# The output staging tile of the second channel matmul: two buffers or three

## Chip, cores, metric

One core of one Trainium2 chip. The metric is device time in microseconds (us) of one execution, median over several executions. On one core a run counts as slow when it lies over 1.5% above the fastest of the same kernel.

## The reference, cut to what matters

Cosine attention over 8 batches, 12 heads, 448 rows, head size 64, followed by a token-and-channel mixer on the 448 x 768 result of each batch.

```python
q_n = q / (norm(q) + 1e-6);  k_n = k / (norm(k) + 1e-6)
attn = softmax(q_n @ k_n.T / tau)
x = (attn @ v)                       # laid out as batch, 448, 768
h = relu(x.T @ w_tok1) @ w_tok2      # token mixing
u = x + h.T
h2 = relu(u @ w_ch1) @ w_ch2         # channel mixing, hidden size 1536
out = u + h2                         # float32
```

The change touches only the last line: the sum `u + h2` and its way to memory.

## The kernel before

The program runs 48 head pairs through a software pipeline (the loop index `i` below is one pair) and feeds the channel matmuls of finished batches into it piece by piece. The buffers:

```python
outp = ctx.enter_context(tc.tile_pool(name="outp", bufs=2))     # the staging tile
ps = ctx.enter_context(tc.tile_pool(name="ps", bufs=2, space=PSUM))   # two banks: psF, psG, pst, some psU
ps2 = ctx.enter_context(tc.tile_pool(name="ps2", bufs=3, space=PSUM))
```

The second channel matmul, its eviction and its store. Matmuls write into PSUM, a memory of its own that is split into banks; the eviction is the VectorE instruction (L407) that adds the residual to such a result and puts the sum into the staging tile. Each output tile holds 128 rows of 768 float32 (3 KiB a partition) and is filled in two halves, `i0:i1` = 0:3 and 3:6:

```python
def m_ch2(b, m, i0, i1, send=False):
    ...
    if i0 == 0:
        ost[0] = outp.tile([P, D], FP32, name=f"ost_{b}_{m}", tag="ost")
        ost[1] = 0
    o, w = ost[0], P * (i1 - i0)
    psF = ps.tile([P, DH], FP32, name=f"psF_{b}_{m}_{i0}", tag="b")
    for ct in range(CT):                       # 12 matmuls               (L404)
        nc.tensor.matmul(psF[:, 0:w], gt[:, ct, lo:lo + P], wc2t[:, ct, P * i0:P * i1], ...)
    nc.vector.tensor_tensor(out=o[...], in0=psF[...], in1=urt[b][...], op=ALU.add)   # eviction (L407)
    if send or i1 == DT:
        if m < NC:
            nc.sync.dma_start(out=out[b, 0:SM]...[m][:, cols], in_=o[:, cols])       # store (L414)
        else: ...                              # the 64 + 64 remainder rows of two batches (L416, L417)
```

Loads, transposes and stores are all issued from one queue, SyncE's, in program order:

```python
for i in range(NP_ALL + 2):
    if i < DMA_FROM:
        loads(i)                  # q, k, v of later pairs (q: L106, k: L109, v: L112)
    if DMA_FROM <= i + 2 < NP_ALL:
        dma_tpose(i + 2)          # query/key transposes (L265)
    ...
    for p in ut_at.get(i, ()):
        u_tpose(p)                # transposes of the residual (L380)
    ...
    feed(...)                     # channel matmuls, evictions and stores, among scores and attention
```

## Time and profile before

| | before |
|---|---|
| median of the first three runs | 394.86 us (394.48 to 395.2) |
| span of the profiled run | 392.9 us |
| TensorE busy | 378.7 us (96%) |
| VectorE busy | 193.5 us (49%) |
| evictions into the staging tile | 57 (28 tiles) |
| of these, held by a store | 1, for 3.4 us |

In a timeline line the columns are start in us from the span's start, length in us, engine, source line, operation, output and inputs, count; in brackets stands how long the engine was idle before it and what released it. "SPq" is the queue that issues the transfers; a line there is the issue, not the moving of the bytes. In a list of waits the columns are who waited for whom, us in total, times, longest.

The prediction shows the main lines. Two more of the kernel before belong to the argument. First, the waits of the issuing queue between 82 and 100 us:

```profile
SPq L106 <- POOL kq L211: 7.4, 1, 7.4
```

A query load (L106) held the queue for 7.4 us, because its buffer was still being read by GpSimd's scaling (L211). Everything behind it in the queue waited too: two transposes, and then the first store, whose tile was full at 82.31, 4.06 us before the load could go out at 86.37. Second, a table by stretches, of 86 to 100 us and 100 to 360 us: for each engine busy us and instructions in brackets, in the order TensorE, weight loads, VectorE, ScalarE, GpSimd; then granted clock, DMA share, GB/s.

```profile
86.00:100.00 14.00, 12.72 (x114) 7.46 (x113) 7.50 (x13) 4.21 (x6) 12.72 (x19) 1.00 1.02 227
100.00:360.00 260.00, 259.85 (x2535) 157.14 (x2534) 117.86 (x232) 145.78 (x247) 136.30 (x191) 1.00 0.77 163
```

TensorE idles 1.28 us in the first stretch and 0.15 us in the 260 us after it.

### The profile page before, as it was taken

How to read it: one execution, taken by the hardware profiler on the slowest of the kernel's cores; microseconds unless marked ns; L12 is line 12 of the kernel's file. 1: busy time of each engine (PE TensorE's matmuls, PEld its weight loads, DVE VectorE, ACT ScalarE, POOL GpSimd, SP SyncE). 2: the span in 40 equal slices, each digit the busy share in tenths (PEclk: the TensorE clock that was granted, in tenths of full speed). 3: DMA queues.
4: the chain of work that ended last, by engine and by line, in shares of the span. 5: the costliest groups of instructions: out<-in, count | busy, mean ns of one | idle time of the engine just before them, and what ended most of it. 6: DMA issues, size and time to landing. Idle time of an engine off the chain costs nothing.

```text
span 392.9 us, 9076 instructions
## 1 busy us (share of the span) xinstructions
PE 378.7 (96%) x3658; PEld 228.5 (58%) x3658; DVE 193.5 (49%) x368; ACT 225.8 (57%) x411; POOL 209.6 (53%) x306
## 2 busy tenths in 40 slices
PE   8678999998999999999999999999999999999996
PEld 3346555665565656566556566566566566565554
DVE  5688758865344554545524645345534342333022
ACT  5998698843774639573676446673775536511400
POOL 4978486789267584868572947659561700000000
PEclk9899999999999999999999999999999999999999
DMA  7999999969968987999989899999982452013013
GB/s 203 276 238 253 246 236 215 227 138 264 209 131 190 202 183 179 222 183 208 205 199 198 175 245 216 166 189 182 242 142 56 123 123 68 16 57 102 5 40 120
DMA packets 137514, 67.51 MB, mean 172 GB/s; under 512 B 93248, under 2 KB 134016, under 8 KB 137472
## 3 DMA queue, kind: packets, MB, share of 16 engines
q1 hardware_dynamic: 133296, 61.36, 71.4%
q0 software_dynamic: 3632, 5.18, 7.4%
q8 instruction: 28, 0.46, 0.5%
q10 hardware_dynamic: 544, 0.39, 0.3%
q14 instruction: 14, 0.11, 0.1%
HBM read 43.38 MB, written 11.01 MB: 138 GB/s over the span
## 4 chain that ended last, share of the span: by engine, by line
PE 86%; ACT 6%; DVE 3%; DMA 2%; SPq 1%; issue 1%; ACTq 0%; DVEq 0%
PE psF L404 28%; PE psG L389 27%; PE psO L320 9%; PE psS L301 7%; PE psR L341 5%; PE psU L361 4%; ACT pt L302 3%; PE psO L322 3%; PE psX L308 2%; DMA out_dram<-ost 1%; DMA km<-in_k_dram 1%; PE psU L366 1%; PE pst L243 1%; ACT sq L178 1%; DVE ost L407 1%
## 5 line engine op out<-in xcount | busy, mean ns | idle before, releaser
L302 ACT ACTIVATE pt<-psS 128x896 f16<-128x896 f32 x141 | 119.0, 921 | 65.8 <-PE psS L301 65.5
L389 PE MATMUL psG<-ut,wc1t 128*128 128x448 f16 x576 | 119.5, 353 | 0.2
L404 PE MATMUL psF<-wc2t,gt 128*128 128x384 f16 (+2 forms) x684 | 117.3, 324 | 1.2 <-DVE ost L407 1.1
L391 ACT ACTIVATE gt<-psG 128x448 f16<-128x448 f32 x96 | 51.1, 557 | 73.2 <-PE psG L389 73.2
L404 PEld LDWEIGHTS <-gt 128*128 128x128 f16 x684 | 64.5, 98 | 48.4 <-issue 8.1
L389 PEld LDWEIGHTS <-wc1t 128*128 128x128 f16 x576 | 53.2, 98 | 52.5 <-issue 8.7
L211 POOL TENSOR_TENSOR kq<-km,rn 128x384 f16<-128x384 f32 x47 | 39.4, 837 | 80.9 <-ACT rn L204 80.7
L407 DVE TENSOR_TENSOR ost<-psF,ur 128x384 f32<-128x384 f32 (+2 forms) x57 | 31.4, 550 | 90.0 <-PE psF L404 86.6
L320 PEld LDWEIGHTS <-pt 128*128 128x128 f16 x1152 | 50.1, 97 | 8.4 <-issue 2.4
L320 PE MATMUL psO<-vt,pt 128*128 128x65 f16 x1152 | 52.4, 193 | 1.2 <-ACT pt L302 0.8
L326 DVE RECIPROCAL rec<-psO 128x8 f32<-128x8 f32 x48 | 9.9, 207 | 80.9 <-PE psO L322 80.9
L193 DVE TENSOR_REDUCE ssq<-sq 128x12 f32<-128x768 f32 (+1 forms) x49 | 45.1, 929 | 5.3 <-ACT sq L178 3.7
L322 PE MATMUL psO<-vx,pt 128*128 128x130 f16 x192 | 41.8, 218 | 0.0
L180 POOL TENSOR_TENSOR sq<-km 128x384 f32<-128x384 f32 x42 | 34.5, 823 | 13.2 <-DMA km<-in_k_dram 13.0
L211 POOL TENSOR_TENSOR kq<-qm,rn 128x384 f16<-128x384 f32 x47 | 39.5, 841 | 0.0
L301 PE MATMUL psS<-qk 64*128 64x448 f16 x282 | 36.1, 357 | 2.0 <-DVE qk L261 0.9
L327 DVE TENSOR_TENSOR x<-psO,rec 128x512 f16<-128x512 f32 x48 | 33.2, 691 | 1.7
L341 PE MATMUL psR<-x,w1t 128*128 128x128 f16 x384 | 29.2, 219 | 0.1
L309 ACT ACTIVATE pt<-psX 128x448 f16<-128x448 f32 x48 | 27.1, 564 | 3.3 <-PE psX L308 2.3
L361 PE MATMUL psU<-w2t,r 128*128 128x448 f16 x96 | 25.9, 353 | 1.5 <-DVE w2t L149 1.1
L180 POOL TENSOR_TENSOR sq<-qm 128x384 f32<-128x384 f32 x30 | 24.7, 822 | 2.4 <-DVE ssq L193 1.6
L341 PEld LDWEIGHTS <-w1t 128*128 128x128 f16 x384 | 23.8, 97 | 2.1 <-issue 0.3
(76 smaller groups left out, 320.8 us busy)
## 6 DMA issues: line engine op xcount, KB each, us to landing
vm<-in_v_dram SPq DMA_DIRECT2D x16, 576.0 KB, 5.0
out_dram<-ost SPq DMA_DIRECT2D x23, 384.0 KB, 3.1
qm<-in_q_dram SPq DMA_DIRECT2D x14, 576.0 KB, 5.1
km<-in_k_dram SPq DMA_DIRECT2D x14, 576.0 KB, 5.6
wc1t<-in_moe_w_ch_dram POOLq DMA_DIRECT2D x2, 1152.0 KB, 13.8
wc2t<-in_moe_w_ch_dram POOLq DMA_DIRECT2D x2, 1152.0 KB, 12.6
out_dram<-ost SPq DMA_DIRECT2D x9, 192.0 KB, 2.7
xq<-in_q_dram SPq DMA_DIRECT2D x7, 192.0 KB, 5.2
```

What stands on the lines that cost most here:

```text
L180: eng.tensor_tensor(out=out, in0=src, in1=src, op=ALU.mult)
L193: nc.vector.tensor_reduce(out=ssqs[p // HP % 3][:, lo + 6 * a0:lo + 6 * a1], in_=sq[p][:, a0:a1].rearrange("p a g e -> p (a g) e"), axis=A ...
L211: eng.tensor_tensor(out=kqs[n % 2][:, j, a, 0:NC, :].rearrange("p c (g e) -> p g c e", g=2), in0=src, in1=_bcast_free(rn, E), op=ALU.mult)
L301: nc.tensor.matmul(psS[:, g, 0:S], qk[r, P * c:P * (c + 1)], qk[r, 512:512 + S], start=True, stop=True)
L302: nc.scalar.activation(out=pt[:, 2 * S * c:2 * S * (c + 1)].rearrange("p (g s) -> p g s", g=2), in_=psS[:, :, 0:S], func=AF.Exp, scale=inv ...
L320: nc.tensor.matmul(psO[:, m, E1 * g:E1 * (g + 1)], pt[:, at:at + P], vt[:, 2 * j + g, c, 0:E1], start=(g == 0 and c == 0), stop=False)
L322: nc.tensor.matmul(psO[:, m, 0:2 * E1], pt[:, PX + P * m:PX + P * (m + 1)], vx[:, j, 0:2 * E1], start=False, stop=True)
L341: nc.tensor.matmul(psR[:, tt, :], w1t[:, m, tt * P:(tt + 1) * P], xs[p][:, m, :], start=(m == 0), stop=(m == NC))
L361: nc.tensor.matmul(psU, rs[p][:, tt, :], w2t[:, tt, lo:lo + S], start=(tt == 0), stop=by_dma and tt == TT - 1)
L389: nc.tensor.matmul(psG[:], wc1t[:, dt, ct * P:(ct + 1) * P], ut[:, dt, sp], start=(dt == 0), stop=(dt == DT - 1))
L391: nc.scalar.activation(out=gt[:, ct, sp], in_=psG[:], func=AF.Relu)
L404: nc.tensor.matmul(psF[:, 0:w], gt[:, ct, lo:lo + P], wc2t[:, ct, P * i0:P * i1], start=(ct == 0), stop=(ct == CT - 1))
```

## The change

The intent is to let a tile be written while two earlier ones are still on their way out.

```diff
-    outp = ctx.enter_context(tc.tile_pool(name="outp", bufs=2))
+    outp = ctx.enter_context(tc.tile_pool(name="outp", bufs=3))
```

## The prediction

> **What bounds the kernel now**
>
> I read the page first, parts 1, 2 and 4: which engine is full, where it is not, and which engine the chain that ended last runs through.
>
> ```profile
> PE 378.7 (96%) x3658; PEld 228.5 (58%) x3658; DVE 193.5 (49%) x368; ACT 225.8 (57%) x411; POOL 209.6 (53%) x306
> ...
> PE   8678999998999999999999999999999999999996
> ...
> PE 86%; ACT 6%; DVE 3%; DMA 2%; SPq 1%; issue 1%; ACTq 0%; DVEq 0%
> ```
>
> TensorE is occupied 96% of the span and carries 86% of the chain. A change of buffers can therefore gain only where TensorE stands still because of a buffer. The busy row shows three such places: the start (slices 1 to 4), one slice further on (the tenth digit is an 8: that slice of 9.8 us runs from 88 to 98 us), and the drain at the end.
>
> Next, the staging tile itself: its view lists what held its writers up and who waited for them.
>
> ```profile
> L407 DVE TENSOR_TENSOR ost<-psF,ur x57: 290/557/559, 78.4 to 389.7; 128x384 f32<-128x384 f32 x55, 128x256 f32<-128x256 f32 x1, 128x128 f32<-128x128 f32 x1
> L414 SPq DMA_DIRECT2D out_dram<-ost x26: 331/356/713, 89.5 to 390.1; - x26
> ...
> its engine sat idle before it (us, times) until:
>   PE psF L404: 86.6, 56
>   DMA out_dram<-ost: 3.4, 1
> who waited for it (us, times):
>   DVE ost L407: 3.4, 1
>   PE psF L404: 1.1, 1
> ```
>
> Of 57 evictions (PSUM plus residual into the tile), 56 waited for the matmul that feeds them, which is as it should be. One waited for a store of the same tile to land: the third tile of the first batch, the first that takes a used buffer. TensorE waited 1.1 us behind it. That is the whole hold of the two buffers on this run.
>
> Last, that place in order of time (VectorE, then the queue that issues the stores, then TensorE):
>
> ```profile
> 81.75 0.56 DVE L407 TENSOR_TENSOR ost<-psF,ur 128x384 f32<-128x384 f32 x1 [0.38 <-PE psF L404]
> ...
> 94.17 0.56 DVE L407 TENSOR_TENSOR ost<-psF,ur 128x384 f32<-128x384 f32 x1 [3.38 <-DMA out_dram<-ost]
> ```
> ```profile
> 86.37 0.37 SPq L106 DMA_DIRECT2D qm<-in_q_dram  x1
> 86.84 2.53 SPq L380 DMA_TRANSPOSE ur<-ut  x2
> 89.46 1.02 SPq L414 DMA_DIRECT2D out_dram<-ost  x2
> ```
> ```profile
> 83.35 0.61 PE L341 MATMUL psR<-x,w1t 128*128 128x128 f16 x8
> 83.79 2.11 PE L404 MATMUL psF<-wc2t,gt 128*128 128x384 f16 x12
> ...
> 93.03 0.61 PE L341 MATMUL psR<-x,w1t 128*128 128x128 f16 x8
> ...
> 94.78 2.11 PE L404 MATMUL psF<-wc2t,gt 128*128 128x384 f16 x12 [1.13 <-DVE ost L407]
> ```
>
> The first tile was full at 81.75 + 0.56 = 82.31, but its store was issued only at 89.46, in a pair with the second tile's. Ahead of it in the same queue stands a query load, which the queue's list of waits shows held 7.4 us for GpSimd's scaling to free its buffer, and two transposes. The chain gives the store 4.61 us to land, 89.46 to 94.07. So a store of ordinary length went out 7.15 us late, and that made two buffers one too few, once.
>
> **What the Trainium skill says**
>
> The page "DMA: Bandwidth & Descriptors", section "Anatomy of one DMA — SWDGE (gpsimd) path", says that the DMA engines wait on no semaphores: the wait is on the issuing sequencer before dispatch. The page describes the GpSimd path there; these stores go out from SyncE, and the trace agrees for that queue: nothing is issued between the load of 78.05 and the one of 86.37 while the first tile lies ready. "Perfetto Trace Analysis", section "Identifying Performance Opportunities", holds that consistent bubbles can mean too little on-chip memory for the next tile. Here the bubble comes once in 57, so I expect one bubble's worth. "PSUM — Partial Sum Buffer", section "Engine vs sequencer instructions", says VectorE's queue is strictly first in, first out, and that matmuls start in program order. The trace agrees: the copy of the transposed queries, whose transposes were done at 91.91 + 0.20 = 92.11, starts at 94.64, behind the held eviction. "SBUF — State Buffer", section "SBUF size: 192, 224, or 256?", gives some 208 KiB usable a partition; adding up the kernel's tile shapes gives about 202 KiB now and 205 KiB with one more 768-element f32 row (3 KiB), so it should fit. No trace shows that.
>
> **The change part by part**
>
> It adds a third buffer of 3 KiB a partition, allocated last of the on-chip pools. It removes no instruction and moves none in program order. Arithmetic, loads and stores stay.
>
> What it takes away: the third tile of batch 0 gets an unused buffer.
> 1. The held eviction. Its matmuls start at 89.27 and are given 2.12 us, ending 91.39. The sister eviction at 88.70 begins 0.04 us after its matmuls (86.55 + 2.11 = 88.66). VectorE is free at 90.04 + 0.74 = 90.78. So it would start at 91.43 in place of 94.17, 2.74 us earlier. The 3.38 us shown count from 90.78, and 0.65 us of them would become a wait for TensorE.
> 2. TensorE. The second half's matmuls at 94.78 need a PSUM bank that the first half holds (two banks are shared there), and they follow the token matmuls at 93.03. Undisturbed, that step takes 83.79 - 83.35 = 0.44 us, one iteration before. Here it took 94.78 - 93.03 = 1.75. The eviction would now be done at 91.99, well before 93.47, so TensorE saves 1.75 - 0.44 = 1.31 us. The view's 1.13 us counts from the modelled end of pipelined matmuls; I take the start-to-start figure.
> 3. The rest of VectorE's 2.74 us is slack: the query copy, reciprocal, normalisation and rectifier move forward, but TensorE needs none of them earlier. The wait for the bank at 97.53 (the 12 matmuls at 94.78 plus one eviction) moves with TensorE.
> 4. All other tiles: 56 evictions wait for TensorE with two buffers already. Gain 0. At the end, the store of the remainder rows is issued at 383.04 and the last tile, reusing its buffer, is first written at 387.76; stores there land in a median of 2.3 us, so 2 us are spare.
>
> Sum: 1.31 us on the path, 0 elsewhere. Does it reach the end? From 101.2 to 360 us the table by stretches shows TensorE busy in all 258.8 us, and no DMA wait of TensorE itself from 97 us on (its weight loads show one of 0.4 us, without loss). So the later work moves forward as a block. 394.86 - 1.31 = 393.55 us, or -0.33%.
>
> **The rivals**
>
> - Given back: a later wait on something that does not move takes the 1.3 us. Candidates are GpSimd and the loads. GpSimd is full from 89.8 to 98.1; its square at 99.06 waits 1.01 us for a VectorE sum, so it can move forward only 1.0 us where TensorE moves 1.3. But GpSimd then waits 9.12 us for ScalarE at 111.03. The query transpose issued at 92.14 is read first by scores at 105.45, and its listed landing time is 6.2 us, so 7 us are spare. Time: 394.9. I give it one in ten, most likely as a part.
> - The whole 3.4 us come home: 391.5. This needs TensorE to have been hurt by VectorE's backlog after 94.17 too. Against it: the token rectifier is done at 96.45 and TensorE asks for its result at 96.72. One in thirty.
> - Bank takes over: the second half now waits for another holder of the two PSUM banks. Against it: the same sequence an iteration earlier, without the DMA wait, has the 0.44 us step. One in thirty.
> - Slower through placement: another address or another semaphore wait costs something. The tile comes last in memory, so I see no mover. One in fifty above 395.3.
>
> **Range and chances**
>
> The runs before spread 394.48 to 395.2, that is 0.36 us either way. Around 393.55 I put 392.9 below (noise plus a small extra), and 394.6 above (noise plus most of the gain lost). Faster by over 2% would need 7.9 us, six times the only wait there is; slower by as much has no cause in sight. So 1%, 98%, 1%; I predict 393.6 us.
>
> **What would show it**
>
> The view of the staging tile should list 57 waits for the matmuls and none for the store, and no TensorE wait for that eviction. The eviction near 94.17 should start near 91.4, and the step from the token matmuls to the second half should fall from 1.75 to 0.44 us. The first store should still be issued near 89.46: the late store is not cured, only no longer waited for. The channel matmuls at 97.53 should start near 96.2 and the drain's evictions (376.06 and on) 1.3 us earlier. Wrong would be: the drain does not move although 97.53 did (given back), or the step at 93 us stays long with another releaser (the bank).

## The result, and the profile after

| | before | after |
|---|---|---|
| median of 5 runs | 394.91 us (394.48 to 395.66) | 393.92 us (393.38 to 394.23) |
| span of the profiled run | 392.9 us | 391.6 us |
| TensorE busy | 378.7 us | 378.7 us |
| evictions that waited for a store | 1 | 0 |
| from the token matmuls to the second half's matmuls | 1.75 us | 0.44 us |

A ratio is the mean time of one kernel's fast runs over the mean of the other's of the same rounds, so not quite the ratio of the medians. Here it is 0.9971, with a 95% interval of 0.9957 to 0.9986: 0.29% of 394.91 us, or 1.15 us, faster. That is clear of the noise, and "same" at the 2% mark.

The staging tile's view of the changed kernel:

```profile
its engine sat idle before it (us, times) until:
  PE psF L404: 87.2, 56
who waited for it (us, times):
```

No eviction waits for a store, and nobody waits for an eviction. VectorE's evictions of the second and third tile, in order of time:

```profile
88.65 0.56 DVE L407 TENSOR_TENSOR ost<-psF,ur 128x384 f32<-128x384 f32 x1 [1.56 <-PE psF L404]
...
91.38 0.56 DVE L407 TENSOR_TENSOR ost<-psF,ur 128x384 f32<-128x384 f32 x1 [0.65 <-PE psF L404]
```

The eviction that stood at 94.17 starts at 91.38 and waits 0.65 us for its matmuls. TensorE behind it, and the store in the queue:

```profile
92.98 0.61 PE L341 MATMUL psR<-x,w1t 128*128 128x128 f16 x8
93.42 2.11 PE L404 MATMUL psF<-wc2t,gt 128*128 128x384 f16 x12
...
96.19 1.30 PE L389 MATMUL psG<-ut,wc1t 128*128 128x448 f16 x6
```
```profile
87.99 0.37 SPq L106 DMA_DIRECT2D qm<-in_q_dram  x1
88.47 3.19 SPq L380 DMA_TRANSPOSE ur<-ut  x2
91.75 1.01 SPq L414 DMA_DIRECT2D out_dram<-ost  x2
```

The step is 93.42 - 92.98 = 0.44 us. The first store goes out even later than before, at 91.75 in place of 89.46, after the evictions into the third tile have begun. It took 2.5 us to land, to 94.25, so with two buffers this run would have stood still about as long as the run before (an estimate from these two figures; the store before landed at 94.07). At the end of the program the evictions that began at 376.06 begin earlier by about the same 1.3 us:

```profile
374.71 0.56 DVE L407 TENSOR_TENSOR ost<-psF,ur 128x384 f32<-128x384 f32 x1 [15.01 <-PE psF L404]
```

### The profile page after: what moved, and what is told of

Its sections match the earlier page's. It is cut to its first block, busy times and chain, and to the rows that moved or that the text cites. A ratio compares the mean times of both kernels' runs of the same rounds, so it can differ in the third digit from the quotient of the medians.

```text
span 391.6 us, 9075 instructions
## 1 busy us (share of the span) xinstructions
PE 378.7 (97%) x3658; PEld 228.9 (58%) x3658; DVE 193.6 (49%) x368; ACT 226.1 (58%) x411; POOL 209.6 (54%) x306
## 4 chain that ended last, share of the span: by engine, by line
PE 88%; ACT 7%; DVE 3%; DMA 1%; issue 1%; SPq 0%; DVEq 0%
PE psF L404 28%; PE psG L389 28%; PE psO L320 9%; PE psS L301 7%; PE psR L341 5%; PE psU L361 4%; ACT pt L302 3%; PE psO L322 3%; PE psX L308 2%; DMA qm<-in_q_dram 1%; PE psU L366 1%; ACT sq L178 1%; PE pst L243 1%; ACT pt L309 1%; ACT rn L203 1%
## 5 line engine op out<-in xcount | busy, mean ns | idle before, releaser
L389 PE MATMUL psG<-ut,wc1t 128*128 128x448 f16 x576 | 119.5, 353 | 0.2
L407 DVE TENSOR_TENSOR ost<-psF,ur 128x384 f32<-128x384 f32 (+2 forms) x57 | 31.4, 550 | 87.2 <-PE psF L404 87.2
L341 PE MATMUL psR<-x,w1t 128*128 128x128 f16 x384 | 29.2, 219 | 0.1
L341 PEld LDWEIGHTS <-w1t 128*128 128x128 f16 x384 | 23.8, 97 | 2.1 <-issue 0.4
```

Of the source, the lines that this page charges most:

```text
L341: nc.tensor.matmul(psR[:, tt, :], w1t[:, m, tt * P:(tt + 1) * P], xs[p][:, m, :], start=(m == 0), stop=(m == NC))
L389: nc.tensor.matmul(psG[:], wc1t[:, dt, ct * P:(ct + 1) * P], ut[:, dt, sp], start=(dt == 0), stop=(dt == DT - 1))
```

## The experiments

Three theories were on the table. **Late store**: the whole gain is one wait, and that wait exists because the first store stands late in the queue. **Placement**: the gain comes from something else, such as the memory taken or luck at the start of the run. **Slow store**: the store's own landing time makes two buffers too few, wherever it stands in the queue. All kernels that ran gave correct results. The first four ran on one chip with eleven shared runs of the kernel before (median 395.32), the next three on one chip with seven (395.24), the last three on one chip with seven (395.27).

**The changed kernel again.** No edit.

> The changed kernel once more, on the chip and in the rounds of the next three runs, so that they can be set against it. Late-store theory (the whole gain is the one wait of the third tile of batch 0 for a store that stood late in its queue): no wait of the evictions for a store, the step from the token matmuls near 93 us to the second half's matmuls 0.44 us, time 1.0 to 1.4 us below before (ratio 0.9965 to 0.9975). Placement theory (the gain comes from something other than that wait, such as the memory taken or start-up luck): the ratio may be anything from 0.995 to 1.0, with no tie to that step.

Measured: 393.68 us median of six executions; ratio of the five fast ones 0.9959 (0.9947 to 0.9971), 1.62 us faster. The gain holds; its size moved from 1.15 to 1.62 us. The profiled execution of this run was an oddity (1344 us, told at the end) and is left out as slow, so the traced parts of this expectation rest on the first trace of the changed kernel alone.

**Two buffers and unused memory.**

```diff
     ost = {}
+    outp.tile([P, D], FP32, name="pad", tag="pad", bufs=1)     # bufs=2 as before
```

> Two buffers as before, and 3 KiB a partition of never used memory in the same pool, so that the pool is as large as with three. Late-store theory: the wait of about 3.4 us and the 1.75 us step are back, time as before within 0.4 us (ratio 0.999 to 1.001). Placement theory: the gain stays, ratio about 0.997.

Measured: 395.55 us median; ratio 1.0013 (1.0000 to 1.0026). The gain is gone and the wait is back, in the staging tile's view:

```profile
  PE psF L405: 86.6, 56
  DMA out_dram<-ost: 3.3, 1
```

The step in this trace is 95.17 - 93.51 = 1.66 us. Memory taken does nothing; placement falls, as far as the pool's size goes.

**Two buffers, the blocking load one iteration later.** This takes away the cause of the late store and leaves the buffers alone.

```diff
-    q_at = at({n: early_qk.get(n, 10 if n == 6 else 3 * n - 9) for n in range(2, NHALF)})
+    q_at = at({n: early_qk.get(n, {6: 10, 7: 13}.get(n, 3 * n - 9)) for n in range(2, NHALF)})
```

> Two buffers; only the query load that stood ahead of the first store in the queue is issued one iteration later. Late-store theory: the first tile's store goes out at 82.4 to 85 us in place of 89.5, lands before 90, the wait for a store is gone, the step is 0.44 us, and two buffers run like three: ratio 0.9965 to 0.9975. Slow-store theory (the store's own landing of some 4.6 us, not its place in the queue, makes two buffers too few): the wait stays in part, over 1 us. Placement theory: time as before.

Measured: 393.6 us median; ratio 0.9961 (0.9948 to 0.9974). The queue, and VectorE's third tile:

```profile
81.14 3.44 SPq L380 DMA_TRANSPOSE ur<-ut  x2
84.67 4.84 SPq L414 DMA_DIRECT2D out_dram<-ost  x2
89.64 0.39 SPq L106 DMA_DIRECT2D qm<-in_q_dram  x1
```
```profile
91.30 0.56 DVE L407 TENSOR_TENSOR ost<-psF,ur 128x384 f32<-128x384 f32 x1 [0.65 <-PE psF L404]
```

The first store goes out at 84.67, the load now stands behind it, and two buffers run as fast as three. This store took 3.6 us to land, and in this trace stores take 1.5 to 5.7 us (before: 1.6 to 5.3), so the slow-store theory falls as the whole cause: with the position in the queue mended, such landings hold nobody up. The landing still counts as a term of the sum. In the trace before it was long, 4.61 us against a median of 2.8; had the late store landed in 2.8 us, at 92.3, the eviction would have ended near 92.9, before the 93.47 at which TensorE wants the bank (an estimate from that trace). In the two-buffer run strictly in turn, below, the store went out at 92.52 and landed in only 2.69 us, and the wait was there all the same: enough lateness does it alone.

**Both at once.** The same edit, with three buffers.

> The later query load and three buffers together. Late-store theory: both take away the same wait, so nothing adds: like e0_again within 0.4 us, ratio 0.9965 to 0.9975. Placement theory, or two separate causes: the gains add, ratio about 0.994.

Measured: 393.78 us median; ratio 0.9967 (0.9955 to 0.9979). Nothing adds. Either edit, or both, removes the same 1.3 to 1.6 us.

**A store held back, two buffers: a miss of mine.** The first tile's store is kept until just ahead of the third tile, so that a longer wait should follow.

```diff
+        if (b, m, i0) == (0, 2, 0):
+            held.pop()()
         if i0 == 0:
             ost[0] = outp.tile([P, D], FP32, name=f"ost_{b}_{m}", tag="ost")
...
-            if m < NC:
+            if (b, m) == (0, 0):
+                held.append(lambda: nc.sync.dma_start(
+                    out=out[b, 0:SM].rearrange("(p c) d -> c p d", c=NC)[m], in_=o[:]))
+            elif m < NC:
```

> Two buffers; the first tile's store is held back on purpose until just ahead of the third tile's first eviction in program order, so that in the queue it comes after the next load, one query transpose and two residual transposes. Those end near 96.9 us in the trace of before. Late-store theory: the store goes out near 97 (to 98.5), lands 3 to 4.6 us later, the third tile's eviction starts at 100 to 103 in place of 94.2, and TensorE's stall grows by the same 6 to 9 us: time 401 to 404 us, ratio 1.015 to 1.023. Rival (the wait is mostly hidden or is given back by slack later): under 3 us longer, ratio below 1.008.

Measured: 395.4 us median; ratio 1.0007 (0.9988 to 1.0025). Neither theory's number: the time stayed that of before. The chain of waits and the queue say why:

```profile
91.57 3.61 DMA out_dram<-ost
...
95.30 0.57 DVE ost L410
```
```profile
91.57 0.53 SPq L420 DMA_DIRECT2D out_dram<-ost  x1
...
97.53 0.35 SPq L417 DMA_DIRECT2D out_dram<-ost  x1
```

The held store (L417) goes out at 97.53, but the third tile is written from 95.30 on, released by the store issued at 91.57 (the second tile's). So the third tile was in the second tile's buffer: here the pool did not hand out its two buffers in turn. The run tests nothing about a longer wait; it only shows the usual one again (TensorE's step 95.91 - 93.76 = 2.15 us).

**The same held store, three buffers.**

> The same held store with three buffers. Late-store theory: nothing waits for it, time as the changed kernel, ratio to before 0.996 to 0.9985, although the store goes out near 97 us. If the held store cost something by itself (queue order, other transfers): slower than before too, ratio above 1.0.

Measured: 393.68 us median; ratio 0.9963 (0.9948 to 0.9978). The held store goes out at 96.65, and all 57 evictions wait for their matmuls alone. Holding the store costs nothing by itself.

**One buffer.**

```diff
-    outp = ctx.enter_context(tc.tile_pool(name="outp", bufs=2))
+    outp = ctx.enter_context(tc.tile_pool(name="outp", bufs=1))
```

> One buffer. Late-store theory: the second tile's first eviction (85.9 us before) waits for the first store to land near 94, a stall of 7 to 8 us for TensorE; the third tile waits 2 to 3 us for the second store; the other 25 reuses wait 0 to 2 us each at the eviction (2.2 us between a full tile and the next first eviction against a landing of 2 to 3 us), most of it hidden by the second PSUM bank. Time 403 to 410 us, ratio 1.02 to 1.04. If instead every reuse cost TensorE its full wait: 27 times 1 to 3 us, over 425 us.

Measured: 413.08 us median; ratio 1.0448 (1.0430 to 1.0467), 17.7 us slower and above my range. The staging tile's view:

```profile
  DMA out_dram<-ost: 62.1, 17
  PE psF L404: 54.3, 28
...
who waited for it (us, times):
  DVE ost L407: 62.1, 17
  PE psF L404: 11.3, 4
...
  PE psG L389: 3.6, 3
```

VectorE stands 62.1 us for stores in 17 places, TensorE only 11.3 + 3.6 = 14.9 us for VectorE: most of the waits don't reach TensorE. That it is the second PSUM bank which hides them is argued, not tried. Apart from the longest, 9.3 us, the waits average (62.1 - 9.3) / 16 = 3.3 us, where I had put 0 to 3. The largest one, for the second tile, cost TensorE 8.2 us against my 7 to 8. What I had not counted: TensorE was busy 384.4 us in place of 378.7, that is 5.7 us more for the same instructions. From 92 to 98 us its granted clock was 0.50, right after the long idle time, and the twelve matmuls there took 4.00 us in place of 2.11. That is about a third of the 5.7 us; the rest was not traced to its places. (The traced execution was the slowest of the four, 415.22 us.)

**Two buffers strictly in turn** (control for the next). Two tags with one buffer each, taken alternately:

```diff
-            ost[0] = outp.tile([P, D], FP32, name=f"ost_{b}_{m}", tag="ost")
+            ost[0] = outp.tile([P, D], FP32, name=f"ost_{b}_{m}", tag=f"ost{ost[2] % 2}", bufs=1)
+            ost[2] += 1
```

> Two buffers named by hand, used strictly in turn (the run before with the held store took the second tile's buffer for the third tile, so it did not test what it was meant to). Control for the next run. Late-store theory: exactly as before, one wait of about 3.4 us, ratio 0.998 to 1.002.

Measured: 395.04 us median; ratio 0.9997 (0.9976 to 1.0017). As before in time. The view lists two waits for stores, 5.3 us in all: the one of 3.76 us near 95, and another of 1.5 us that no TensorE wait follows.

**The held store, two buffers strictly in turn.** The two edits above together.

> Two buffers strictly in turn, and the first tile's store held back as in the run before, so that the third tile has to wait for it. Late-store theory: the store goes out at 96.5 to 98.5 us, lands 3 to 4.6 us later, the third tile's eviction starts at 100 to 102.5, TensorE's stall grows by 6 to 8.5 us; the run with one buffer showed that an idle time of 8 us is followed by some microseconds at half the granted clock, which I put at 2 to 4 us more. Time 402 to 407 us, ratio 1.018 to 1.03. Rival (a longer wait is hidden or given back by slack further on): ratio below 1.01.

Measured: 402.35 us median; ratio 1.0183 (1.0155 to 1.0211), 7.2 us slower: far outside the noise, though "unclear" at the 2% mark, which lies inside the interval. The queue, VectorE and TensorE in order of time, and the table by stretches:

```profile
96.71 0.36 SPq L418 DMA_DIRECT2D out_dram<-ost  x1
```
```profile
99.47 0.56 DVE L411 TENSOR_TENSOR ost<-psF,ur 128x384 f32<-128x384 f32 x1 [8.83 <-DMA out_dram<-ost]
```
```profile
92.89 0.61 PE L341 MATMUL psR<-x,w1t 128*128 128x128 f16 x8
100.08 4.00 PE L408 MATMUL psF<-wc2t,gt 128*128 128x384 f16 x12 [6.58 <-DVE ost L411]
103.88 0.95 PE L361 MATMUL psU<-w2t,r 128*128 128x448 f16 x2
```
```profile
94.00:98.00 4.00, 0.00 (x0) 0.00 (x0) 0.00 (x0) 0.00 (x0) 3.96 (x5) 1.00 1.09 282
98.00:102.00 4.00, 1.92 (x7) 0.88 (x7) 2.25 (x5) 0.00 (x0) 0.32 (x1) 0.51 0.17 66
```

The step is 100.08 - 92.89 = 7.19 us, so 7.19 - 0.44 = 6.75 us of stall. The twelve matmuls then take 103.88 - 100.08 = 3.80 us to the next group, where the changed kernel takes 95.38 - 93.42 = 1.96, at a granted clock near 0.5: 1.84 us more. Up to the channel matmuls at 104.95 it is 4.87 us in place of 96.19 - 93.42 = 2.77, so 2.10 us more in all. Together 8.85 us; the spans of the two profiled runs differ by 400.4 - 391.6 = 8.8. Against the kernel before, the store goes out 96.71 - 89.46 = 7.25 us later but lands quicker (2.67 us in the chain of waits, against 4.61). So the eviction starts 99.47 - 94.17 = 5.3 us later, and the step grows by 7.19 - 1.75 = 5.4 us: a later landing passes into TensorE's stall one for one, plus a toll of 2.1 us after the long idle. Later slack gave nothing back. With the quicker landing the eviction came earlier than I expected (99.47, not 100 to 102.5) and the stall grew less (5.4 us, not 6 to 8.5).

**The held store, three buffers strictly in turn.** The held store as above, with the index modulo 3.

> The same held store with three buffers strictly in turn. Late-store theory: no wait for a store though it goes out near 97 us, time as the changed kernel, ratio 0.995 to 0.9985. If the held store itself costs time: above 1.0.

Measured: 393.75 us median; ratio 0.9961 (0.9938 to 0.9983). No eviction waits for a store. The held store, and the third tile's eviction before it:

```profile
98.28 0.35 SPq L418 DMA_DIRECT2D out_dram<-ost  x1
```
```profile
92.14 0.56 DVE L411 TENSOR_TENSOR ost<-psF,ur 128x384 f32<-128x384 f32 x1 [0.65 <-PE psF L408]
```

The same delay that costs 7.2 us with two buffers costs nothing with three.

**Four buffers** could not be built: the pool would need 12 KiB a partition, and the allocator reported 11.8125 KiB left for it. Three take 9 of these. With the 202 KiB that the prediction counts for two buffers, this makes 202 - 6 + 11.8 = 207.8 KiB in all, which bears out the prediction's 208.

**A check over all traces.** The token matmuls near 93 us (L341) start between 92.89 and 93.79 us in the traces of the kernels with two or three buffers, the slow one left out, so up to 0.9 us of a run's time is settled before the change can act. Counted from there to the end of the span, the five traces without the wait take 298.60 to 298.67 us. The four with the usual wait take 299.79 (unused memory), 299.87 (before), 300.31 (strictly in turn) and 300.34 us (first held store). Their steps lie 1.22, 1.31, 1.68 and 1.71 us above 0.44; with that taken off, 298.56 to 298.63 us are left. So the step is the whole difference to within 0.1 us, and nothing else that differs between these programs shows in the time after 93 us.

No kernel here beats the changed one: the blocking load moved with two buffers equals it, within the intervals, and takes 3 KiB a partition less.

## Why the prediction was right

Forecast 393.6 us in a range of 392.9 to 394.6; measured 393.92 us. Point by point:

- **One wait, one place.** Right. The wait vanished with the third buffer, came back with unused memory in its stead, and vanished again with two buffers when its cause was moved. One word was loose: the 4.61 us of that store were not "ordinary length" (the median was 2.8 us, 3.1 for stores of its size), and by the estimate given with the moved load the loss in that trace needed both the late issue and the long landing.
- **The held eviction to start at 91.43, 2.74 us earlier.** 91.38, 2.79 us earlier; 0.65 us of the wait turned into one for the matmuls, as worked out.
- **TensorE's step to fall to 0.44 us, worth 1.31 us.** 0.44 in the trace, and the span shrank by 1.3 us. On the clock the gain was 1.15 us in the first set and 1.62 us in the second. The four traces in which two buffers show the usual wait tell why it is not one number: their steps are 1.75 (before), 1.66 (unused memory), 2.15 (first held store, which in effect waited as usual) and 2.12 us (strictly in turn), so 1.2 to 1.7 us each above 0.44. The forecast read it from one trace, and that it came so near the measured gain is in part luck.
- **The first store still near 89.46.** Off: 91.75, because the query load ahead of it went out 1.6 us later and the two transposes took 0.7 us longer to issue. It did not matter, which is what the third buffer buys.
- **Moves forward as a block.** Right. The channel matmuls begin at 96.19 (forecast near 96.2), the drain at 374.71 in place of 376.06.
- **57 waits for the matmuls.** 56 are listed; one eviction, at 82.77, found both VectorE and its operands ready. A miss of no weight.
- **The rivals.** Given back: no; TensorE is busy 260.00 of 260 us from 100 to 360 us in the changed kernel too. The whole 3.4 us: no. The bank takes over: no. Slower through placement: no sign, and the unused-memory run and the check over all traces speak against it.

What the runs add to the forecast: the late store as the cause was only argued there, from the order of issue. Moving the load shows it, and holding the store shows that lateness is what counts.

What stays open: why the pool took the second tile's buffer for the third tile in the first held run was read from the trace, not looked up; and a gain of 1.15 or 1.62 us is not told apart by these intervals.

## What to carry to other kernels

In this kernel a buffer was worth the waits that the tile's own view lists, and of these only the part that the full engine waits behind: 1.3 of 3.4 us, and with one buffer some 15 of 62 us. Before adding a buffer for stores, look at what stands ahead of the store in its issuing queue; here a load that waited for its own buffer, with two transposes behind it, held a finished store for 7.15 us, and moving the load did the same for no memory. Issuing the stores from another queue was not tried. A long stall of TensorE cost more than its length: 2.1 us on top of 6.75.

## What the Trainium skill lacked or had wrong

- "TensorE: Matmul & The Clock Gate" in the Trainium skill, section "What's actually happening": it says the clock goes to half after at least one idle window of about 3.4 us. The runs agree: after 6.58 and 8.20 us of idle the granted clock was 0.51 and 0.50, after idle of 1.1 to 1.5 us it was 1.00. It also says that whatever is issued in the first 3.4 us or so runs slow and everything after it at full speed. In the held run the slow stretch was longer, about 4.9 us (the matmuls from 100.08 are slow, those from 104.95 take their usual 1.30 us), so the 3.4 us served here as a lower bound.
- One execution of the changed kernel took 1344.47 us: its channel matmuls took 992 ns each in place of 353 ns, 425.9 us in all in place of 119.5, yet the granted clock was recorded as 1.00. The same page, section "Seeing it yourself", warns that the clock gate's records have been unreliable and that the clock has been seen stuck at a quarter (K=1/4) for 50 us and more. That may be what happened; here the slowness lasted the whole 1342.7 us, and no run shows the cause. It came once; the five other executions of that set took 393.3 to 394.07 us.
- "DMA: Bandwidth & Descriptors", section "Anatomy of one DMA — SWDGE (gpsimd) path", says the wait sits on the issuing sequencer, but puts no cost on what stands behind it. Here one load waiting for its buffer, and the two transposes behind it, held a finished tile's store 7.15 us, and in the held run a landing 5.3 us later reached TensorE as 5.4 us more stall. SyncE's stores of 384 KB landed in a median of 3.1 us here, the first one in 4.61 us before and in 2.5 us after; the fit given there is for GpSimd's path only.
